# One K tile with rows of 64 KB in a decode kernel: fewer, larger loads, and the buffers that wait for them

## Chip, cores and metric

The kernel runs on one core of one Trainium2 chip, alone on that chip. The metric is the device time of one execution in microseconds.

## The reference, cut to what matters

```python
# x: [2, 1, 512]; k_cache, v_cache: [2, 32, 8192, 128] bf16, 134 MB each; wq [512, 4096], wo [4096, 512]
q = (layernorm(x) @ wq) per head
p = softmax(q . k * 128**-0.5)          # one query row per batch and head, 8192 keys
h = x + (p @ v) @ wo
out = h + relu_gated_ffn(layernorm(h))  # W_gate, W_up [512, 1376], W_down [1376, 512]
```

Almost all bytes are the two caches. Each is read once, with one multiply-add per element and query.

Of the kernel before, what the change touches and what calls it, by code (L numbers as in the profile page):

```python
# [8 lines left out]
BF16 = mybir.dt.bfloat16  # L9
# [30 lines left out]
def bass_sequential_preLN__gqa_block_cached__glu_gated_reglu__decode_kernel(  # L40
# [16 lines left out]
    DC = D // 128  # L57
# [22 lines left out]
    with ExitStack() as es:  # L80
# [15 lines left out]
        v_sem = [S(f"v{i}") for i in range(2)]  # L96
# [9 lines left out]
        K = [sb(f"K{i}", [128, SLOT], BF16) for i in range(2)]  # L106
# [14 lines left out]
        onesn = sb("onesn", [128, 128], BF16)  # L121
        scr = prod[:].rearrange("p j d -> p (j d)")
# [46 lines left out]
        def k_rows(p):  # L169
            hq, b = divmod(p // 2, B)  # L170
            return A_k_cache[b, A * hq:A * hq + A].rearrange(
                "h (p k j) d -> k (h p) (j d)", p=128 // A, k=2)[p % 2]

        def v_rows(o):
            hq, b = divmod(o, B)
            return A_v_cache[b, A * hq:A * hq + A].rearrange("h (p j) d -> (h p) (j d)", p=128 // A)

        def tile(x, p):
            return x[:].rearrange("p (k j d) -> p k j d", j=J, d=Dh)[:, p % 2 if x is V else 0]

        if True:

            def program():

                def load_k(p):
                    nc.sync.dma_start(K[p % 2][:], k_rows(p)).then_inc(k_sem[p % 2], 16)

                def load_v(o, k0, k1, sem):
                    nc.sync.dma_start(V[:, k0 * Dh:k1 * Dh], v_rows(o)[:, k0 * Dh:k1 * Dh]).then_inc(sem, 16)
# [5 lines left out]
                load_k(0)  # L195
                load_k(1)
# [104 lines left out]
                for r in range(2):  # L301
# [16 lines left out]
                load_v(0, 0, 2 * J, v_sem[0])  # L318
                nc.sync.dma_start(
                    X[:], A_wo[0:128 * DR].rearrange("(p r) n -> p (r n)", r=DR)).then_inc(sem_wo, 16)  # L320
# [41 lines left out]
                nc.tensor.sem_inc(v_sem[1], 16 * (NI - 1))  # L362
# [12 lines left out]
                body = Tokens(pe.count)  # L375

                def k_part(T, p, ev, k_wait):
                    k_t = tile(K[p % 2], p)
# [3 lines left out]
                    def score(g):  # L382
                        wait(a2p, ev[g])
                        kv_ = kT[g % 2][:].rearrange("p (k n r) -> p k r n", n=128, r=2)
                        for k in range(GT // 2):
                            jj = g * GT + 2 * k
                            for r in range(2):
# [3 lines left out]
                                if loop and g == NG - 2 and k == r == 0:  # L391
                                    T.mark(("kf", p), i)
# [23 lines left out]
                def pv(T, p, parts, between=None):  # L416
# [18 lines left out]
                    T.mark(("pv", p), i)  # L435
# [24 lines left out]
                with nc.Fori(0, NI, engines=OrderedEngineSet([nc.tensor.engine])):  # L460
                    k_part(body, 0, (1, 2, 3, 4), ((k2p, 1),))
                    collect(body, 6)
                    k_part(body, 1, (8, 9, 10, 11), ((k2p, 2),))
                    pv(body, 0, ((JC, J, ((v_sem[0], 16),)), (0, JC, ())))
                    pv(body, 1, ((JC, J, ((v_sem[1], 16), (a2p, 12))), (0, JC, ((a2p, EV),))))
# [4 lines left out]
                    for sem in v_sem:  # L470
                        nc.tensor.sem_inc(sem, -16)
                    nc.tensor.sem_inc(k2p, -2)
# [4 lines left out]
                tail = Tokens(0)  # L477
# [12 lines left out]
                pv(tail, P0, ((JC, J, ((v_sem[0], 16),)), (0, JC, ((a2p, 13),))))  # L490
# [64 lines left out]
                def q_copy(o):  # L555
                    if o == 0:
                        pool.wait(t_q2, t_q_b)
                    else:
                        pool.wait(tokp("fp", 2 * o - 2), (d2s, 2 * o))
                    nc.gpsimd.tensor_copy(out=q_c[:], in_=q_all[:, o]).then_inc(g2d, 1)  # L560

                def k_mult(p):
                    return nc.vector.tensor_tensor(  # L563
                        out=prod[:, 0:JC, :], in0=tile(K[p % 2], p)[:, 0:JC, :],
                        in1=q_c[:, Q2:QW].unsqueeze(1).broadcast_to([128, JC, Dh]), op=ALU.mult)

                def k_adds(p, run, last):
                    w = Dh
                    while w > 8:
# [3 lines left out]
                            out=prod[:, 0:JC, 0:w], in0=prod[:, 0:JC, 0:w], in1=prod[:, 0:JC, w:2 * w], op=ALU.add))  # L573
                    last()

                def k_reduce(p):
                    return nc.vector.tensor_reduce(  # L577
                        out=scores[p % PG][:, 0:JC], in_=prod[:, 0:JC, 0:8], axis=AX.X, op=ALU.add)
# [17 lines left out]
                with nc.Fori(0, NI, engines=OrderedEngineSet([nc.vector.engine])):  # L596
# [9 lines left out]

                    for q in range(PG):
                        if q == 0:
                            nc.vector.wait_ge(g2d, 1)
# [266 lines left out]
```

## The kernel before, the parts that the change touches

Work goes in 16 items. An item is one batch and four heads: 8 MB of K and 8 MB of V. The 128 partitions hold 256 positions each. K comes as two halves of 128 positions in two tiles, V as one tile of rows of 64 KB.

```python
K = [sb(f"K{i}", [128, SLOT], BF16) for i in range(2)]   # 32 KB a partition each
V = sb("V", [128, 2 * SLOT], BF16)                       # 64 KB a partition
X = sb("X", [128, DR * D], BF16)                         # wo, 28 KB a partition, loaded second after V(0)
prod = sb("prod", [128, JC, Dh], BF16)                   # 24 KB, VectorE's product
```

Of each half, VectorE makes the scores of positions 0 to 95 (product with q, four halving adds, a reduce). TensorE makes those of the other 32 (transposes, copies by ScalarE, matmuls). VectorE's loop body goes half by half:

```python
for q in range(PG):                       # the two halves
    if q == 0: nc.vector.wait_ge(g2d, 1)
    nc.vector.wait_ge(k_sem[q], 16)
    nc.vector.sem_inc(k2p, 1)             # lets TensorE start on this half
    run_d(k_mult(q))
    last_d(); nc.vector.sem_inc(d2s, 1)   # VectorE no longer needs this half of K
    k_adds(q, run_d, last_d)
    if q == 0:
        nc.vector.wait_ge(p2d, 1); normalize(Ob, run_d, last_d); run_d(o_scale(O_cur[:])); ...
    run_d(k_reduce(q))
    last_d(); nc.vector.sem_inc(d2a, 1)   # ScalarE may take the exps
```

SyncE issues each half of K as soon as VectorE and TensorE are through with the half that it replaces, and V when the last matmul on the old V is through:

```python
if p + 2 < NP:                             # p counts halves
    sp.wait((d2s, p + 1), tokp("kf", p))
    load_k(p + 2)
if p % 2 == 1 and p < P0 - 3:
    sp.wait(tokp("pv", p))
    load_v(p // 2 + 1, 0, 2 * J, v_sem[0])
# ... the last two items come in pieces (cut)
```

The softmax here doesn't subtract the row's maximum and nothing guards it: scores larger than these inputs give would overflow.

## Time and profile before

| What | Before |
|---|---|
| time, median of the first 3 runs | 658.9 us (658.81 to 659.58) |
| one period of the loop (an item) | 38.78 us in every one of 13 periods, to 0.01 |
| bytes of a period, and rate | 16.78 MB, 432.6 GB/s |
| VectorE busy in a period | 28.8 us |

Ways to read it: the row of DMA tenths tells how full the 16 DMA engines are. A transfer in the chain of waits is drawn from its issue to its landing, so most of a long one is time spent behind other transfers. In this text the "lead" of a load is the time from its issue to the landing of the load queued before it. The lines themselves are in the prediction.

### The profile page before, as it was taken

How to read it: one execution, taken by the hardware profiler on the slowest of the kernel's cores; microseconds unless marked ns; L12 is line 12 of the kernel's file. 1: busy time of each engine (PE TensorE's matmuls, PEld its weight loads, DVE VectorE, ACT ScalarE, POOL GpSimd, SP SyncE). 2: the span in 40 equal slices, each digit the busy share in tenths (PEclk: the TensorE clock that was granted, in tenths of full speed). 3: DMA queues.
4: the chain of work that ended last, by engine and by line, in shares of the span. 5: the costliest groups of instructions: out<-in, count | busy, mean ns of one | idle time of the engine just before them, and what ended most of it. 6: DMA issues, size and time to landing. Idle time of an engine off the chain costs nothing.

```text
span 657.5 us, 7820 instructions
## 1 busy us (share of the span) xinstructions
PE 306.7 (47%) x3096; PEld 202.9 (31%) x3097; DVE 469.1 (71%) x275; ACT 274.0 (42%) x687; POOL 25.5 (4%) x96
## 2 busy tenths in 40 slices
PE   2644345444354445436444443644445354445466
PEld 0331232323233232323314232331323233133234
DVE  1594594958949496794949769494985949589881
ACT  1642343433454254344424534442454435335271
POOL 4000000000000000000000000000000000002000
PEclk9856557655575755557565575756557575556676
DMA  9999999999999999999999999999999999999997
GB/s 383 422 437 430 437 439 419 470 391 447 425 462 433 403 447 415 470 397 439 445 419 458 403 447 417 443 441 423 443 419 462 405 437 447 417 429 433 429 421 310
DMA packets 8629, 281.17 MB, mean 428 GB/s; under 512 B 966, under 2 KB 1068, under 8 KB 1580
## 3 DMA queue, kind: packets, MB, share of 16 engines
q1 hardware_dynamic: 8612, 281.06, 99.3%
q8 instruction: 5, 0.08, 0.1%
q14 instruction: 4, 0.03, 0.0%
q10 hardware_dynamic: 8, 0.00, 0.0%
HBM read 281.05 MB, written 0.00 MB: 427 GB/s over the span
## 4 chain that ended last, share of the span: by engine, by line
DMA 80%; DVE 15%; PE 3%; issue 1%; ACT 0%; DVEq 0%; SPq 0%
DMA K<-in_A_k_cache_dram 69%; DVE prod L563 15%; DMA V<-in_A_v_cache_dram 5%; DMA K<-in_B_W_gate_dram 4%; DMA V<-in_A_wq_dram 2%; PE T L345 1%; PE O L428 1%; PE O L272 1%; ACT kT L589 0%; PE O L775 0%; PE O L827 0%; PE O L330 0%; PE Ob L440 0%; PE T L405 0%; DVE prod L281 0%
## 5 line engine op out<-in xcount | busy, mean ns | idle before, releaser
L563 DVE TENSOR_TENSOR prod<-K,q_c 128x12288 bf16<-128x12288 bf16 x32 | 209.9, 6558 | 146.7 <-DMA K<-in_A_k_cache_dram 136.0
L572 DVE TENSOR_TENSOR prod<-prod 128x6144 bf16<-128x6144 bf16 (+3 forms) x128 | 212.2, 1658 | 7.8
L405 PE MATMUL T<-ident_f,K 128*128 128x128 f32 x512 | 123.3, 403 | 134.6 <-DVEq L611 134.6
L589 ACT ACTIVATE kT<-T 128x1024 bf16<-128x1024 bf16 x128 | 127.1, 1022 | 122.7 <-PE T L405 118.7
L428 PE MATMUL O<-V,e 128*16 128x512 bf16 x1024 | 91.4, 533 | 111.8 <-DMA V<-in_A_v_cache_dram 111.8
L517 ACT ACTIVATE e<-scores 32x96 bf16<-32x96 f32 x128 | 53.9, 421 | 196.5 <-DVEq L625 193.3
L405 PEld LDWEIGHTS T<-ident_f,K 128*128 128x128 f32 x512 | 88.6, 206 | 137.6 <-DVEq L611 137.5
L428 PEld LDWEIGHTS O<-V,e 128*16 128x16 bf16 x1024 | 30.5, 117 | 165.3 <-DMA V<-in_A_v_cache_dram 113.3
L388 PE MATMUL S<-q_c,kT 128*128 128x8 bf16 x1024 | 48.6, 171 | 44.8 <-ACT kT L589 44.6
L388 PEld LDWEIGHTS S<-q_c,kT 128*128 128x128 bf16 x1024 | 41.9, 107 | 73.1 <-ACT kT L589 71.3
L440 PE MATMUL Ob<-sel,os_sb 128*128 128x4 f32 x136 | 30.2, 345 | 38.4 <-ACT os_sb L592 38.4
L440 PEld LDWEIGHTS Ob<-sel,os_sb 128*128 128x128 f32 x136 | 28.7, 312 | 40.3 <-ACT os_sb L592 40.2
L517 ACT ACTIVATE e<-S 32x32 bf16<-32x32 f32 x128 | 29.8, 233 | 16.1 <-PE S L388 15.0
L577 DVE TENSOR_REDUCE scores<-prod 128x96 f32<-128x768 bf16 x32 | 30.5, 953 | 2.8
L517 ACT ACTIVATION_READ_ACCUMULATOR e<-scores 32x1 f32 x128 | 30.0, 235 | 0.0
L517 ACT ACTIVATION_READ_ACCUMULATOR e<-S 32x1 f32 x128 | 25.6, 200 | 1.5
L589 ACT ACT_TABLE_LOAD x15 | 19.2, 1283 | 0.3
L560 POOL COPY q_c<-q_all 128x144 bf16<-128x144 bf16 x16 | 7.5, 472 | 243.5 <-PE O L428 231.3
L592 ACT ACTIVATE os_sb<-O 128x512 f32<-128x512 f32 x17 | 10.1, 597 | 15.3 <-PE O L428 14.9
L544 POOL MEMSET O_l<- 128x32 bf16 x13 | 1.7, 130 | 299.8 <-DVEq L622 299.8
L281 DVE CAST prod<-O 128x512 bf16<-128x512 f32 x1 | 0.7, 692 | 11.0 <-PE O L272 11.0
L272 PE MATMUL O<-V,xlT 128*2 128x512 bf16 x32 | 3.4, 600 | 7.7 <-DMA V<-in_A_wq_dram 7.7
(103 smaller groups left out, 94.2 us busy)
## 6 DMA issues: line engine op xcount, KB each, us to landing
K<-in_A_k_cache_dram SPq DMA_DIRECT2D x32, 4096.0 KB, 29.2
V<-in_A_v_cache_dram SPq DMA_DIRECT2D x3, 4096.0 KB, 31.7
V<-in_A_wq_dram SPq DMA_DIRECT2D x1, 4096.0 KB, 12.3
X<-in_A_wo_dram SPq DMA_DIRECT2D x1, 3584.0 KB, 46.2
V<-in_A_v_cache_dram SPq DMA_DIRECT2D x1, 3072.0 KB, 23.1
K<-in_B_W_up_dram SPq DMA_DIRECT2D x1, 1376.0 KB, 23.6
K<-in_B_W_gate_dram SPq DMA_DIRECT2D x1, 1376.0 KB, 26.6
V<-in_A_v_cache_dram SPq DMA_DIRECT2D x1, 1024.0 KB, 25.2
```

Source lines behind the costliest of these rows:

```text
L272: mm = nc.tensor.matmul(Op[i][32 * t:32 * t + B, :], lhsT=lT[:, c * B:(c + 1) * B], rhs=wq[:, c, n:n + 512], start=(c == 0), stop=(c == DC ...
L388: i = nc.tensor.matmul(Sp[p % 2][:, A * jj:A * jj + 2 * A], lhsT=kv_[:, k, r, :], rhs=q_c[:, 2 * A * r:2 * A * r + 2 * A], start=(r == 0), ...
L405: i = nc.tensor.transpose(Tp[g % 2][:, k * 128:(k + 1) * 128], k_t[:, j:j + 2, :].rearrange("p j d -> p (j d)").bitcast(F32), ident_f[:])
L428: i = nc.tensor.matmul(Op[0][c:c + 16, :], lhsT=e_t[q][:, j // VJ, :], rhs=v_t[:, j:j + VJ, :].rearrange("p j d -> p (j d)"), start=(q == ...
L440: i = nc.tensor.matmul(Ob[:, 0:A], lhsT=os_sb[:, jj * Dh:(jj + 1) * Dh], rhs=sel[:, A * jj:A * jj + A], start=(jj == 0), stop=(jj == VJ - 1))
L517: i = nc.scalar.activation(out=e_t[q][h, j0 // VJ:j1 // VJ, :].rearrange("p g (j a) -> p g j a", a=A)[:, :, :, a], in_=src(h, a), func=ACT ...
L560: nc.gpsimd.tensor_copy(out=q_c[:], in_=q_all[:, o]).then_inc(g2d, 1)
L563: return nc.vector.tensor_tensor(out=prod[:, 0:JC, :], in0=tile(K[p % 2], p)[:, 0:JC, :], in1=q_c[:, Q2:QW].unsqueeze(1).broadcast_to([128 ...
L572: run(nc.vector.tensor_tensor(out=prod[:, 0:JC, 0:w], in0=prod[:, 0:JC, 0:w], in1=prod[:, 0:JC, w:2 * w], op=ALU.add))
L577: return nc.vector.tensor_reduce(out=scores[p % PG][:, 0:JC], in_=prod[:, 0:JC, 0:8], axis=AX.X, op=ALU.add)
L589: to_pe(nc.scalar.activation(out=kT[gg % 2][:], in_=Tp[gg % 2][:].bitcast(BF16), func=ACT.Copy))
L592: to_pe(nc.scalar.activation(out=os_sb[:], in_=Op[0][:], func=ACT.Copy))
```

## The change

The intent: K loads like V, 8 MB in one go with rows of 64 KB, which halves its packets. For this the whole K tile must come free at once. So VectorE makes both halves' products first. The second product needs a place, which is the tile of wo, and wo therefore loads near the end. ScalarE takes the exps of VectorE's scores of both halves last, so that TensorE's second half isn't held up behind them.

```diff
-        K = [sb(f"K{i}", [128, SLOT], BF16) for i in range(2)]
+        K = sb("K", [128, 2 * SLOT], BF16)
+        prods = [X[:, 0:JC * Dh].rearrange("p (j d) -> p j d", d=Dh), prod]
...
-                    for q in range(PG):
-                        if q == 0:
-                            nc.vector.wait_ge(g2d, 1)
-                        nc.vector.wait_ge(k_sem[q], 16)
-                        nc.vector.sem_inc(k2p, 1)
-                        ... (mult, adds, normalise if q == 0, reduce)
+                    nc.vector.wait_ge(g2d, 1)
+                    nc.vector.wait_ge(k_sem[0], 16)
+                    nc.vector.sem_inc(k2p, 1)
                     for q in range(PG):
+                        run_d(k_mult(q, prods[q]))
+                    last_d()
+                    nc.vector.sem_inc(d2s, 1)
+                    nc.vector.wait_ge(p2d, 1)
+                    normalize(Ob, run_d, last_d)
+                    ...
+                    for q in range(PG):
+                        k_adds(prods[q], run_d, last_d)
+                        run_d(k_reduce(q, prods[q]))
...
                         exp_pe(q)
                         if q == 0:
                             sums()
+                    for q in range(PG):
                         nc.scalar.wait_ge(d2a, q + 1)
                         exp_dve(q)
...
-                    if p + 2 < NP:
-                        sp.wait((d2s, p + 1), tokp("kf", p))
-                        load_k(p + 2)
+                    if p % 2 == 1 and p < P1:
+                        o = p // 2 + 1
+                        sp.wait((d2s, 2 * o - 1), tokp("kf", p))
+                        if o < NI:
+                            load(K, A_k_cache, o, k_sem[0])
+                            sp.wait(tokp("pv", p))
+                            load(V, A_v_cache, o, v_sem)
+                        else:   # last item: K half, wo into X, K half, V in pieces
+                            ...
```

More of the change, by code (lines that the diff above doesn't have):

```diff
@@ L95, in bass_sequential_preLN__gqa_block_cached__glu_gated_reglu__decode_kernel @@
         k_sem = [S(f"k{i}") for i in range(2)]
-        v_sem = [S(f"v{i}") for i in range(2)]
+        v_sem = S("v")
         a2p, k2p, l2p = S("a2p"), S("k2p"), S("l2p")
@@ L167, in bass_sequential_preLN__gqa_block_cached__glu_gated_reglu__decode_kernel, with kv_rows, load @@
         ZC = 64
-        def k_rows(p):
-            hq, b = divmod(p // 2, B)
-            return A_k_cache[b, A * hq:A * hq + A].rearrange(
-                "h (p k j) d -> k (h p) (j d)", p=128 // A, k=2)[p % 2]
-        def v_rows(o):
+        def kv_rows(cache, o):
             hq, b = divmod(o, B)
-            return A_v_cache[b, A * hq:A * hq + A].rearrange("h (p j) d -> (h p) (j d)", p=128 // A)
+            return cache[b, A * hq:A * hq + A].rearrange("h (p j) d -> (h p) (j d)", p=128 // A)
         def tile(x, p):
-            return x[:].rearrange("p (k j d) -> p k j d", j=J, d=Dh)[:, p % 2 if x is V else 0]
+            return x[:].rearrange("p (k j d) -> p k j d", j=J, d=Dh)[:, p % 2]
         if True:
             def program():
-                def load_k(p):
-                    nc.sync.dma_start(K[p % 2][:], k_rows(p)).then_inc(k_sem[p % 2], 16)
-                def load_v(o, k0, k1, sem):
-                    nc.sync.dma_start(V[:, k0 * Dh:k1 * Dh], v_rows(o)[:, k0 * Dh:k1 * Dh]).then_inc(sem, 16)
+                def load(x, cache, o, sem, k0=0, k1=2 * J):
+                    nc.sync.dma_start(
+                        x[:, k0 * Dh:k1 * Dh], kv_rows(cache, o)[:, k0 * Dh:k1 * Dh]).then_inc(sem, 16)
                 nc.scalar.dma_start(x_row, A_x[:, 0]).then_inc(sem_x, 16)
@@ L194, in program @@
                     wo_rows, A_wo[128 * DR:].rearrange("(p r) n -> p (r n)", r=4)).then_inc(sem_wl, 16)
-                load_k(0)
-                load_k(1)
+                load(K, A_k_cache, 0, k_sem[0])
                 pool.run(nc.gpsimd.memset(ident_f[:], 0.0))
@@ L317, in program @@
                 sp.wait(t_q)
-                load_v(0, 0, 2 * J, v_sem[0])
-                nc.sync.dma_start(
-                    X[:], A_wo[0:128 * DR].rearrange("(p r) n -> p (r n)", r=DR)).then_inc(sem_wo, 16)
+                load(V, A_v_cache, 0, v_sem)
                 t_mm, t_cp = {}, {}
@@ L361, in program @@
                                  start=True, stop=True)
-                nc.tensor.sem_inc(v_sem[1], 16 * (NI - 1))
                 EV = 13
@@ L373, in mark @@
                         self.at[key] = pe.run(inst)[1] - self.base
-                body = Tokens(pe.count)
+                body, tail = Tokens(pe.count), Tokens(0)
                 def k_part(T, p, ev, k_wait):
-                    k_t = tile(K[p % 2], p)
+                    k_t = tile(K, p)
                     wait = nc.tensor.wait_ge
@@ L390, in score @@
                                     rhs=q_c[:, 2 * A * r:2 * A * r + 2 * A], start=(r == 0), stop=(r == 1))
-                                if loop and g == NG - 2 and k == r == 0:
+                                if loop and p % 2 and g == NG - 2 and k == r == 0:
                                     T.mark(("kf", p), i)
@@ L434, in pv @@
                             n += 1
-                    T.mark(("pv", p), i)
+                    if T is tail or q:
+                        T.mark(("pv", p), i)
                 def collect(T, a):
@@ L462, in program @@
                     collect(body, 6)
-                    k_part(body, 1, (8, 9, 10, 11), ((k2p, 2),))
-                    pv(body, 0, ((JC, J, ((v_sem[0], 16),)), (0, JC, ())))
-                    pv(body, 1, ((JC, J, ((v_sem[1], 16), (a2p, 12))), (0, JC, ((a2p, EV),))))
+                    k_part(body, 1, (7, 8, 9, 10), ())
+                    pv(body, 0, ((JC, J, ((v_sem, 16),)), (0, JC, ((a2p, 12),))))
+                    pv(body, 1, ((JC, J, ()), (0, JC, ((a2p, EV),))))
                     z_sum(Ob)
@@ L469, in program @@
                     nc.tensor.sem_inc(l2p, -1)
-                    for sem in v_sem:
-                        nc.tensor.sem_inc(sem, -16)
-                    nc.tensor.sem_inc(k2p, -2)
+                    nc.tensor.sem_inc(v_sem, -16)
+                    nc.tensor.sem_inc(k2p, -1)
                     nc.tensor.sem_inc(a2p, -EV)
@@ L475, in program @@
                 pe.count = body.base + NI * n_body
-                tail = Tokens(0)
                 P0, P1 = NP - 2, NP - 1
@@ L489, in program @@
                 tail.mark("op", i)
-                pv(tail, P0, ((JC, J, ((v_sem[0], 16),)), (0, JC, ((a2p, 13),))))
+                pv(tail, P0, ((JC, J, ((v_sem, 16),)), (0, JC, ((a2p, 13),))))
                 nc.tensor.wait_ge(a2p, 14)
@@ L558, in q_copy, with k_mult, k_adds @@
                     else:
-                        pool.wait(tokp("fp", 2 * o - 2), (d2s, 2 * o))
+                        pool.wait(tokp("fp", 2 * o - 2), (d2s, 2 * o - 1))
                     nc.gpsimd.tensor_copy(out=q_c[:], in_=q_all[:, o]).then_inc(g2d, 1)
-                def k_mult(p):
+                def k_mult(p, pr):
                     return nc.vector.tensor_tensor(
-                        out=prod[:, 0:JC, :], in0=tile(K[p % 2], p)[:, 0:JC, :],
+                        out=pr[:, 0:JC, :], in0=tile(K, p)[:, 0:JC, :],
                         in1=q_c[:, Q2:QW].unsqueeze(1).broadcast_to([128, JC, Dh]), op=ALU.mult)
-                def k_adds(p, run, last):
+                def k_adds(pr, run, last):
                     w = Dh
@@ L572, in k_adds, with k_reduce @@
                         run(nc.vector.tensor_tensor(
-                            out=prod[:, 0:JC, 0:w], in0=prod[:, 0:JC, 0:w], in1=prod[:, 0:JC, w:2 * w], op=ALU.add))
+                            out=pr[:, 0:JC, 0:w], in0=pr[:, 0:JC, 0:w], in1=pr[:, 0:JC, w:2 * w], op=ALU.add))
                     last()
-                def k_reduce(p):
+                def k_reduce(p, pr):
                     return nc.vector.tensor_reduce(
-                        out=scores[p % PG][:, 0:JC], in_=prod[:, 0:JC, 0:8], axis=AX.X, op=ALU.add)
+                        out=scores[p % PG][:, 0:JC], in_=pr[:, 0:JC, 0:8], axis=AX.X, op=ALU.add)
                 def exp_pe(p):
@@ L605, in last_d @@
                             nc.vector.wait_ge(d2d, n_d[0])
+                    nc.vector.wait_ge(g2d, 1)
+                    nc.vector.wait_ge(k_sem[0], 16)
+                    nc.vector.sem_inc(k2p, 1)
                     for q in range(PG):
-                        if q == 0:
-                            nc.vector.wait_ge(g2d, 1)
-                        nc.vector.wait_ge(k_sem[q], 16)
-                        nc.vector.sem_inc(k2p, 1)
-                        last_d()
-                        run_d(k_mult(q))
-                        last_d()
-                        nc.vector.sem_inc(d2s, 1)
-                        k_adds(q, run_d, last_d)
-                        if q == 0:
-                            nc.vector.wait_ge(p2d, 1)
-                            normalize(Ob, run_d, last_d)
-                            run_d(o_scale(O_cur[:]))
-                            last_d()
-                            nc.vector.sem_inc(d2g, 1)
-                        run_d(k_reduce(q))
+                        run_d(k_mult(q, prods[q]))
[3 more added lines that the diff above has]
+                    normalize(Ob, run_d, last_d)
+                    run_d(o_scale(O_cur[:]))
+                    last_d()
+                    nc.vector.sem_inc(d2g, 1)
+                    for q in range(PG):
+                        k_adds(prods[q], run_d, last_d)
+                        run_d(k_reduce(q, prods[q]))
                         last_d()
                         nc.vector.sem_inc(d2a, 1)
-                    for sem, n in ((d2d, n_d[0]), (g2d, 1), (p2d, 1), (k_sem[0], 16), (k_sem[1], 16)):
+                        if q == 0:
+                            nc.vector.sem_inc(d2s, 1)
+                    for sem, n in ((d2d, n_d[0]), (g2d, 1), (p2d, 1), (k_sem[0], 16)):
                         nc.vector.sem_inc(sem, -n)
@@ L660, in program @@
                         dve.last()
-                        t_dm[p] = dve.run(k_mult(p))
-                        k_adds(p, dve.run, dve.last)
+                        t_dm[p] = dve.run(k_mult(p, prod))
+                        k_adds(prod, dve.run, dve.last)
                         if p == P0:
-                            dve.wait(tokp("pv", p - 2))
-                        t_s[p] = dve.run(k_reduce(p))
+                            dve.wait(tokp("pv", p - 1))
+                        t_s[p] = dve.run(k_reduce(p, prod))
                         if p == P0:
@@ L697, in program @@
                         exp_dve(p)
-                    if p + 2 < NP:
-                        sp.wait((d2s, p + 1), tokp("kf", p))
-                        load_k(p + 2)
-                    if p % 2 == 1 and p < P0 - 3:
-                        sp.wait(tokp("pv", p))
-                        load_v(p // 2 + 1, 0, 2 * J, v_sem[0])
-                    elif p == P0 - 3:
-                        sp.wait(tokp("pv", p))
-                        load_v(NI - 1, 0, J, v_sem[0])
-                    elif p == P0 - 2:
-                        load_v(NI - 1, J, 2 * J, v_sem[1])
-                    elif p == P0 - 1:
-                        sp.wait(tokp("pv", p - 1))
-                        load_v(NI, 0, J, v_sem[0])
-                        sp.wait(tokp("pv", p))
-                        for k, (j0, j1) in enumerate(((V_LAST, J), (0, V_LAST))):
-                            load_v(NI, J + j0, J + j1, sem_vl[k])
+                    if p % 2 == 1 and p < P1:
[6 more added lines that the diff above has]
+                        else:
+                            load(K, A_k_cache, o, k_sem[0], 0, J)
+                            sp.wait((d2s, 2 * o))
+                            nc.sync.dma_start(
+                                X[:], A_wo[0:128 * DR].rearrange("(p r) n -> p (r n)", r=DR)).then_inc(sem_wo, 16)
+                            load(K, A_k_cache, o, k_sem[1], J, 2 * J)
+                            sp.wait(tokp("pv", p))
+                            load(V, A_v_cache, o, v_sem, 0, J)
+                            for k, (j0, j1) in enumerate(((V_LAST, J), (0, V_LAST))):
+                                load(V, A_v_cache, o, sem_vl[k], J + j0, J + j1)
                     if p == NP - 2:
@@ L719, in program @@
                             nc.sync.dma_start(
-                                K[0][:, k * DC * F:(k + 1) * DC * F],
+                                K[:, k * DC * F:(k + 1) * DC * F],
                                 w.rearrange("(p c) n -> p (c n)", c=DC)).then_inc(sem_w[k], 16)
@@ L723, in program @@
                             nc.sync.dma_start(
-                                K[0][:, 2 * DC * F + r0 * D:2 * DC * F + (r0 + n) * D],
+                                K[:, 2 * DC * F + r0 * D:2 * DC * F + (r0 + n) * D],
                                 B_W_down[r0 * 128:(r0 + n) * 128].rearrange("(p r) n -> p (r n)", r=n)).then_inc(sem_wd[k], 16)
@@ L758, in program @@
                     in1=Sp[0][:, 0:B].unsqueeze(1).broadcast_to([128, DC, B]), op=ALU.subtract))
-                wup, wgt = (K[0][:, k * DC * F:(k + 1) * DC * F].rearrange("p (c f) -> p c f", c=DC)
+                wup, wgt = (K[:, k * DC * F:(k + 1) * DC * F].rearrange("p (c f) -> p c f", c=DC)
                             for k in range(2))
-                wdn = K[0][:, 2 * DC * F:2 * DC * F + 10 * D].rearrange("p (r n) -> p r n", n=D)
+                wdn = K[:, 2 * DC * F:2 * DC * F + 10 * D].rearrange("p (r n) -> p r n", n=D)
                 pe.wait(t_d)
```

## The prediction

> **What bounds the kernel now.** I read the page's slices first, then the chain of waits, then one steady period of the loop in windows and in the timeline, and last the two ends of the span. The slices say what is full:
>
> ```profile
> DVE  1594594958949496794949769494985949589881
> DMA  9999999999999999999999999999999999999997
> GB/s 383 422 437 430 437 439 419 470 391 447 425 462 433 403 447 415 470 397 439 445 419 458 403 447 417 443 441 423 443 419 462 405 437 447 417 429 433 429 421 310
> DMA packets 8629, 281.17 MB, mean 428 GB/s; under 512 B 966, under 2 KB 1068, under 8 KB 1580
> ```
>
> The reader is to see that the DMA row is 9 in every slice but the last, while VectorE, the busiest engine, is between. The chain of waits, in order of time, repeats one piece from 72.9 us to 577.0 us, here for two rounds and for its end:
>
> ```profile
> 189.36 6.57 DVE prod L563
> ...
> 196.00 32.02 DMA K<-in_A_k_cache_dram
> ...
> 228.14 6.57 DVE prod L563
> ...
> 577.17 6.57 DVE prod L563
> ...
> 583.81 0.33 SPq L186
> 584.14 0.06 issue
> 584.20 31.70 DMA V<-in_A_v_cache_dram
> 615.90 0.04 issue
> ```
>
> It looks as if VectorE's product (6.57 us) sat in a loop with the K load. It does not: those 32.02 us for 4 MB are mostly queueing behind what was issued earlier. One item (K as two 4 MB halves, V as 8 MB) takes 38.78 us, and the windows of one period, and of the one where V too came as two halves, show the DMA engines full throughout and VectorE at 28.8 of 38.78:
>
> ```profile
> 189.24:228.02 38.78, 16.70 (x174) 11.54 (x174) 28.79 (x15) 16.71 (x42) 1.02 (x5) 0.60 1.00 432
> 577.04:615.82 38.78, 15.73 (x136) 11.10 (x136) 36.66 (x17) 15.38 (x41) 3.73 (x5) 0.54 1.01 432
> ```
>
> (columns: stretch, its length, busy PE, PE load, DVE, ACT, POOL, granted clock, DMA share, GB/s). 16,777,216 bytes in 38.78 us are 432.6 GB/s. So bytes set the end, as long as the queue never runs dry. How deep it is shows in the timeline of the same period:
>
> ```profile
> 196.00 15.74 SPq L186 DMA_DIRECT2D K<-in_A_k_cache_dram  x2
> ...
> 218.36 4.91 PE L428 MATMUL O<-V,e 128*16 128x512 bf16 x64 [6.94 <-DMA V<-in_A_v_cache_dram]
> ...
> 223.31 0.33 SPq L189 DMA_DIRECT2D V<-in_A_v_cache_dram  x1
> ```
>
> K's first half is issued at 196.0 while V, landing at 218.3, is still in flight; V is issued at 223.3 with both halves of K still to come (the first lands at 228.0, the second 9.7 us later). There are always 10 to 22 us of work in the queue.
>
> **What the Trainium skill says.** (1) "DMA: Bandwidth & Descriptors", section "Where 436 GB/s comes from": 16 ports give 435.2 GB/s. The trace agrees: 432.6 is 99.4% of that, so better loads alone can win 0.6% at most. (2) Same page, "Why small descriptors are slow (HBM only)": a packet has a small fixed overhead that matters for descriptors of a few hundred bytes. At 32 and 64 KB the trace shows almost nothing of it (below). (3) "VectorE: DVE Perf Modes", section on the mode that packs two bf16 into one read: two results a cycle at 0.96 GHz. The product of 12,288 elements would then take 6.40 us; the trace has 6.558. Changing the buffer that it writes should not change that. (4) "SBUF — State Buffer", "Who interferes with whom": a VectorE instruction with two SBUF inputs and a GpSimd one that reads SBUF exclude each other. The trace of before cannot confirm it, as GpSimd's few instructions (0.13 to 0.30 us each) lie beside the reduce, which has one input.
>
> **The change part by part.**
>
> *Rows of 64 KB for K.* A period has per DMA engine 16 packets for K (8 per half) and 8 for V. Against the ceiling of 435.2 (38.55 us) the period loses 0.23 us, 0.23/24 = 9.6 ns a packet. A second view: the period with V in halves ended at 615.90 instead of 577.04 + 38.78 = 615.82, so 0.08 us for 8 more packets an engine, 10 ns each. The change takes away 8 packets an engine for each of 15 items (the last keeps its halves), and 8 more where V was split in item 14: 16 x 0.08 = 1.3 us gained, an estimate.
>
> *wo moves from second in the queue to the end.* 3.67 MB take 8.5 us of the queue wherever they stand. Nothing starts on it before the tail. 0 us.
>
> *Order of VectorE.* Same instructions: two products, eight adds, two reduces, three small ones. 0 us of work, but their order now sets when buffers come free, and the queue is shallower, as the whole 8 MB of K are held until both halves are used. I lay one new period out from the moment K lands (0), with the durations of the old one.
> - K free for VectorE: start 0.12, two products of 6.56 back to back: 13.3.
> - K free for TensorE: first half's transposes and scores as now (0.09 to 6.2), exps to 8.2, copy of the sums to 8.8, collect to 10.7 (in the old period at 228.02 it ran 236.84 to 238.71), and the last transposes of the second half are through when its third score group starts, 4.67 after its own start (228.11 to 232.78): 15.4. Today the second half waits for VectorE; now it need not.
> - So K(next) is issued at about 15.45. V lands at 19.4 (8.39 MB at 432.6 GB/s). An issue must come ahead of the landing before it by start plus completion latency: the first load of the kernel took 12.32 us for 9.70 us of bytes, so 2.63. Deadline 16.75; slack 1.3 us.
> - V free: products to 13.3, normalise to 14.1, adds 6.8 and reduce 1.0 to 21.9, again to 29.8, exps of the second half 1.9 to 31.7 (old: 257.98 to 259.83), last 24 matmuls in four column groups, 6 x 0.43 = 2.6 at half clock, and V(next) is issued at 34.6 (33.3 at full clock). K lands at 38.75, deadline 36.1; slack 1.5 us.
>
> Both slacks are positive, so the queue still never runs dry: 0 us lost, and the period stays about 38.7.
>
> *The ends.* At the start K's first data is whole at 33.8 instead of 24.1, but VectorE had 9 us of idle per period and V is issued as before at 16.6. At the end the order is K first half, wo, K second half, V in pieces, weights; wo is issued 22 us after the landing of item 14's K, with 7 us of queue left, V's first part at 34.6 with 12 us left. The second half of K still lands 19.4 us before the last V piece (VectorE needs 6.6 + 6.7 + 1.0 and exps 1.9 = 16.2), and the feed-forward weights come last as now, landing at about 655. 0 us.
>
> Sum: 658.9 - 1.3 = 657.6; I keep back 0.2 for jitter in the thin slacks: 657.8 us.
>
> **The rivals.**
> 1. *The queue runs dry once a period*, at the issue of K or of V. For it: slacks of 1.3 and 1.5 us beside sums of 15 and 35 us, and a latency measured once, on an empty machine. GpSimd's reads (point 4 above) now lie beside adds with two SBUF inputs and could hold VectorE up by 0.5 to 0.8 us. Against it: the adds are not on the path to K's release, and V's slack takes 0.8. Each microsecond of deficit costs some 14 to 15 us: 1 us late makes 672.
> 2. *Larger rows are worth more*, near the ceiling: 15 x 0.23 = 3.5 us, so 655.4. Against it: K's 4 MB landed 9.7 us after V did, at the same rate as V's 64 KB rows.
> 3. *VectorE becomes the bound*, now that both products come ahead of everything. It has 28.8 of 38.78 us and starts with K's landing; its last reduce at 29.8 leaves 9 us. Against the clock it is safe: 0 us.
>
> **Range and chances.** Without a dry queue the time lies in 655.5 to 659.5, and the ceiling rules out a gain of 2% (646). A partial shortage of 0.2 to 0.3 us a period would give 661 to 662. For 2% slower (672) a deficit of 0.9 us in all periods is needed, that is an error of over 2 us in my layout: 8%. Range 656.0 to 662.0; faster 0.01, same 0.91, slower 0.08.
>
> **What would show it right or wrong.** Right: a period of 38.7 between K landings, DMA share 1.00 in each, SyncE issuing K about 15.5 and V 33 to 34.6 after a landing, products at 6.56. Wrong: periods above 38.8 with a DMA share below 1.00; then the lateness of the K issue (after 16.8) or of the V issue (after 36.1) says which slack was mis-sized, and if both issues are on time, the latency of 2.63 was. A period below 38.6 would speak for rival 2.

## The result, and the profile after

The changed kernel took 668.9 us (median of 6 runs, 664.8 to 670.9), against 658.9 (658.5 to 659.6, 6 runs). The ratio is 1.014, with a 95% interval of 1.011 to 1.017. Ratios here are the mean time of one kernel's fast runs over that of the other's in the same rounds, so they are not quite the ratio of the medians. The loss is under 2%, but beyond the noise and outside the predicted range. The runs also scatter over 6 us where those of before scatter over 1. The profiled execution took 666.1 us, among the faster ones.

The page hardly shows it: the DMA row is the same row of nines. The packets have fallen as intended, and the chain of waits has changed its make-up. First the page before, then the page after:

```profile
DMA 80%; DVE 15%; PE 3%; issue 1%; ACT 0%; DVEq 0%; SPq 0%
```

```profile
DMA packets 6324, 281.16 MB, mean 423 GB/s; under 512 B 710, under 2 KB 812, under 8 KB 1324
DMA 60%; PE 21%; ACT 12%; DVE 4%; issue 1%; SPq 0%; DVEq 0%; ACTq 0%
```

Before, DMA and VectorE's product alternated in the chain, and the DMA's part was queueing. Now the chain goes through TensorE and ScalarE, whose transposes, copies and exps set when K is issued. The time itself is seen in the windows of single periods of the changed kernel (from one landing of K to the next; columns as in the prediction):

```profile
35.06:75.46 40.40, 20.13 (x174) 12.51 (x174) 28.71 (x15) 16.48 (x42) 0.43 (x1) 0.50 1.01 427
75.46:114.17 38.71, 19.92 (x174) 12.53 (x174) 28.71 (x15) 16.64 (x42) 5.46 (x3) 0.54 0.99 422
114.17:153.50 39.33, 20.13 (x174) 12.49 (x174) 28.70 (x15) 16.64 (x42) 5.87 (x5) 0.50 1.00 427
153.50:193.87 40.37, 20.13 (x174) 12.50 (x174) 28.72 (x15) 16.64 (x42) 5.46 (x5) 0.54 1.01 425
...
428.53:467.27 38.74, 20.13 (x174) 12.50 (x174) 28.72 (x15) 16.64 (x42) 5.46 (x5) 0.50 1.00 433
```

The shortest period, 38.70 us, is what was predicted. But it is not every period: the 14 range up to 40.4, and their mean is 39.27. VectorE has the same 28.7 us in each. The DMA share says 1.00 even in a period of 40.4 us. That is the trap of this view: a packet that takes longer than it need counts as busy.

The timeline of the first of these periods (products of VectorE, issues of SyncE, the first matmul on V):

```profile
35.17 6.56 DVE L552 TENSOR_TENSOR X<-K,q_c 128x12288 bf16<-128x12288 bf16 x1 [14.54 <-DMA K<-in_A_k_cache_dram]
41.64 6.55 DVE L552 TENSOR_TENSOR prod<-K,q_c 128x12288 bf16<-128x12288 bf16 x1
...
50.37 0.33 SPq L182 DMA_DIRECT2D K<-in_A_k_cache_dram  x1
54.29 1.03 PE L418 MATMUL O<-V,e 128*16 128x512 bf16 x8 [2.69 <-DMA V<-in_A_v_cache_dram]
...
69.39 0.33 SPq L182 DMA_DIRECT2D V<-in_A_v_cache_dram  x1
75.58 6.56 DVE L552 TENSOR_TENSOR X<-K,q_c 128x12288 bf16<-128x12288 bf16 x1 [10.82 <-DMA K<-in_A_k_cache_dram]
```

K landed at 35.06, and the next K was issued 15.31 us later (15.47 in the following periods; predicted 15.45). V was issued 34.33 us after the landing (predicted 33.3 to 34.6). Both issues were on time by the prediction's layout. K's lead was 54.25 - 50.37 = 3.88 us, and in this period it was not enough: K landed 21.2 us after V, where 8 MB take 19.35. V's lead, in a period without loss, is 38.70 - 34.33 = 4.37 us.

The trace also holds the time at which each of the 16 DMA engines reports each transfer, and the start and duration of each packet. Summed over the 14 periods, K landed 7.0 us later than 19.35 after V, and V 1.1 us later than 19.35 after K. So 86% of the loss is at K. Landings of one transfer over its 16 engines, as offsets from the last in us (from the trace's records):

```
before, K half at 266.80   -2.06 -1.91 -1.90 -1.85 -1.84 -1.83 -1.81 -1.76 -1.73 -1.63 -1.60 -1.54 -1.48 -1.38 -0.38 0
before, K half at 305.57   -2.05 -1.91 -1.88 -1.85 -1.84 -1.82 -1.80 -1.75 -1.71 -1.63 -1.59 -1.51 -1.46 -1.37 -0.37 0
after,  V at 54.25         -1.79 -1.73 -1.65 -1.64 -1.63 -1.61 -1.40 -1.38 -1.37 -1.36 -1.35 -1.34 -1.32 -1.29 -1.26 0
after,  K at 75.46         -2.89 -2.73 -2.68 -2.65 -2.59 -2.46 -2.16 -2.10 -2.03 -1.72 -1.58 -1.55 -1.26 -0.97 -0.95 0
```

Before, the engines end up to 2 us apart, but the pattern repeats to some 0.03 us from period to period. There every load of the loop is issued 12.9 us or more ahead, so no engine waits. After, the pattern changes from one transfer to the next. The packet records around the issue at 50.37 show how. The engines finish V between 52.00 and 53.79, most of them before 52.5. The first packet of the new K starts at 52.16 (1.8 us after the issue). About half of the engines go on with K at once, and the others have to wait, the last of them until 53.57 (3.2 us after the issue). And of the 27 packets that start between 52.15 and 56.3, 20 take over 2.5 us, up to 3.69, instead of 2.42. Of the packets of 64 KB, 261 of 3,840 are long (over 2.5 us) in the changed kernel, 1 of 1,792 in the kernel before, and 25 of 3,840 in run e5 below, which has the same packets. The long packets hold most of the loss: what packets took beyond 2.42 us comes to 0.48 us per engine and period in the changed kernel and 0.07 in e5, while the periods differ by 0.57. That leaves some 0.15 us for waiting, an estimate.

One more thing moved that costs nothing. GpSimd's groups before and after:

```profile
L549 POOL COPY rsel<-rows 128x112 bf16<-128x112 bf16 x14 | 3.9, 276 | 32.4 <-DVEq L622 31.6
L551 POOL TENSOR_TENSOR O_l<-O_cur,mask 128x32 bf16<-128x32 bf16 x14 | 3.4, 241 | 0.0
```

```profile
L538 POOL COPY rsel<-rows 128x112 bf16<-128x112 bf16 x14 | 44.1, 3150 | 35.0 <-DVEq L607 34.1
L540 POOL TENSOR_TENSOR O_l<-O_cur,mask 128x32 bf16<-128x32 bf16 x14 | 25.0, 1785 | 0.0
```

The same instructions take 3.15 us instead of 0.28, since they now lie beside VectorE's adds, which have two inputs in SBUF. The Trainium skill's page "SBUF — State Buffer", section "Who interferes with whom", says that two such instructions contend. Here it is GpSimd that is held up, and not VectorE, whose 28.7 us a period are unchanged.

### The profile page after: what moved, and what is told of

Its sections match the earlier page's. It is cut to its first block, busy times and chain, and to the rows that moved or that the text cites. A ratio compares the mean times of both kernels' runs of the same rounds, so it can differ in the third digit from the quotient of the medians.

```text
span 664.9 us, 7713 instructions
## 1 busy us (share of the span) xinstructions
PE 339.6 (51%) x3096; PEld 210.9 (32%) x3097; DVE 467.9 (70%) x275; ACT 273.2 (41%) x687; POOL 85.6 (13%) x96
## 4 chain that ended last, share of the span: by engine, by line
DMA 60%; PE 21%; ACT 12%; DVE 4%; issue 1%; SPq 0%; DVEq 0%; ACTq 0%
DMA K<-in_A_k_cache_dram 55%; PE T L395 12%; ACT kT L578 7%; DMA K<-in_B_W_down_dram 5%; PE Ob L431 4%; ACT e L506 4%; PE S L378 4%; ACT os_sb L581 1%; DVE prod L561 1%; DVE X L561 1%; DVE X L552 1%; DVE prod L552 1%; PE O L418 0%; DVE scores L566 0%; SPq L713 0%
## 5 line engine op out<-in xcount | busy, mean ns | idle before, releaser
L552 DVE TENSOR_TENSOR X<-K,q_c 128x12288 bf16<-128x12288 bf16 x15 | 98.4, 6559 | 150.0 <-DMA K<-in_A_k_cache_dram 150.0
L418 PE MATMUL O<-V,e 128*16 128x512 bf16 x1024 | 114.3, 611 | 156.8 <-ACT e L506 112.6
L395 PE MATMUL T<-ident_f,K 128*128 128x128 f32 x512 | 131.3, 424 | 75.1 <-DVEq L598 69.9
L395 PEld LDWEIGHTS T<-ident_f,K 128*128 128x128 f32 x512 | 98.2, 224 | 77.2 <-DVEq L598 72.0
L561 DVE TENSOR_TENSOR prod<-prod 128x6144 bf16<-128x6144 bf16 (+1 forms) x68 | 112.7, 1658 | 5.5 <-DVE scores L566 3.7
L552 DVE TENSOR_TENSOR prod<-K,q_c 128x12288 bf16<-128x12288 bf16 x17 | 111.4, 6552 | 3.6 <-DMA K<-in_A_k_cache_dram 2.8
L561 DVE TENSOR_TENSOR X<-X 128x6144 bf16<-128x6144 bf16 (+3 forms) x60 | 99.5, 1659 | 3.8
L538 POOL COPY rsel<-rows 128x112 bf16<-128x112 bf16 x14 | 44.1, 3150 | 35.0 <-DVEq L607 34.1
L540 POOL TENSOR_TENSOR O_l<-O_cur,mask 128x32 bf16<-128x32 bf16 x14 | 25.0, 1785 | 0.0
L566 DVE TENSOR_REDUCE scores<-prod 128x96 f32<-128x768 bf16 x17 | 16.2, 953 | 0.6
```

Source lines behind the costliest of these rows:

```text
L395: i = nc.tensor.transpose(Tp[g % 2][:, k * 128:(k + 1) * 128], k_t[:, j:j + 2, :].rearrange("p j d -> p (j d)").bitcast(F32), ident_f[:])
L418: i = nc.tensor.matmul(Op[0][c:c + 16, :], lhsT=e_t[q][:, j // VJ, :], rhs=v_t[:, j:j + VJ, :].rearrange("p j d -> p (j d)"), start=(q == ...
L538: e.tensor_copy(out=rsel[:, :, o % B, :], in_=bass.AP(x.tensor, x.offset, [list(x.ap[0]), [DR - OS, A], [1, DR]]))
L540: e.tensor_tensor(out=w, in0=O_cur[:].unsqueeze(2).broadcast_to([128, A, NM]), in1=mask[:, off // 4:off // 4 + OS // 4 * (A - 1) + 1:OS // ...
L552: return nc.vector.tensor_tensor(out=pr[:, 0:JC, :], in0=tile(K, p)[:, 0:JC, :], in1=q_c[:, Q2:QW].unsqueeze(1).broadcast_to([128, JC, Dh] ...
L561: run(nc.vector.tensor_tensor(out=pr[:, 0:JC, 0:w], in0=pr[:, 0:JC, 0:w], in1=pr[:, 0:JC, w:2 * w], op=ALU.add))
```

## The experiments

Theory A: a load issued less than about 4.5 us ahead of the landing before it lets some DMA engines run dry. They restart late and with slow packets, and the lateness is no longer the same on each engine, so the slowest engine of one transfer is held up by another's delay in the next. Theory B: the transfers with rows of 64 KB are at fault by their size. Theory C: VectorE's new order or GpSimd's long instructions slow the transfers. Each experiment is the changed kernel with the edit shown. All gave correct results.

| Run | Time, median (range) in us | Ratio to before (95%) |
|---|---|---|
| changed kernel | 668.9 (664.8 to 670.9) | 1.014 (1.011 to 1.017) |
| e1 K as two transfers, same moment | 668.7 (665.7 to 675.1) | 1.018 (1.013 to 1.023) |
| e2 K's first half early | 661.2 (660.8 to 666.6) | 1.004 (1.002 to 1.006) |
| e3 K issued one score group later | 675.8 (673.6 to 679.3) | 1.025 (1.021 to 1.030) |
| e4 collect behind the second half | 660.9 (658.6 to 661.6) | 1.002 (1.000 to 1.004) |
| e5 e4, and normalise last | 657.9 (657.7 to 658.3) | 0.998 (0.997 to 1.000) |
| e6 e4, and V's first half early | 659.3 (658.9 to 660.5) | 1.001 (1.000 to 1.002) |
| e7 only V's first half early | 666.1 (663.8 to 670.2) | 1.011 (1.008 to 1.014) |
| e8 e6 with K as two transfers | 660.0 (659.8 to 660.3) | 1.002 (1.000 to 1.003) |

The kernel before ran beside them at 658.9 us. Runs e1 to e4 and e5 to e8 shared a chip each.

### e1: rows of 32 KB, issued at the same moment

```diff
-                            load(K, A_k_cache, o, k_sem[0])
+                            load(K, A_k_cache, o, k_sem[0], 0, J)
+                            load(K, A_k_cache, o, k_sem[0], J, 2 * J)
     (the same for item 0; VectorE waits for 32 instead of 16)
```

> Changed kernel, but K of an item comes as two transfers of 32 KB rows issued one right behind the other at the point where the one of 64 KB rows was issued. Theory A (the issue comes too late: 3.9 us ahead of the landing of V for the slowest DMA engine and about 2 us for the fast ones, so engines run dry and restart slowly): the issue time is the same, so still slow, 666 to 672 us, K periods 39.0 to 40.4. Theory B (the rows of 64 KB are the cause, by their size): back to 658 to 660 us, every period 38.78.

668.7 us: as slow as the changed kernel. (Its interval straddles 2%, so it is unclear whether it is slower by that much; slower than before it is.) One of its long periods:

```profile
113.30:153.17 39.87, 19.95 (x174) 12.54 (x174) 28.71 (x15) 16.65 (x42) 5.46 (x5) 0.54 1.00 422
```

K has the packets of the kernel before again, and the loss is still there. Theory B falls. The moment of issue and the new order of the engines (theory C) are left.

### e2: the first half of K issued early

```diff
                     for q in range(PG):
                         run_d(k_mult(q, prods[q]))
-                    last_d()
-                    nc.vector.sem_inc(d2s, 1)
+                        last_d()
+                        nc.vector.sem_inc(d2s, 1)
...
+                            sp.wait((d2s, 3 * o - 2), tokp("kf", p - 1))
+                            load(K, A_k_cache, o, k_sem[0], 0, J)
+                            sp.wait((d2s, 3 * o - 1), tokp("kf", p))
+                            load(K, A_k_cache, o, k_sem[0], J, 2 * J)
```

> As the run before, but the first half of K is issued as soon as its product and its transposes are done, about 6.8 us after K has landed, and the second half at 15.5 us as before. Theory A: the queue never has less than 12 us ahead of it when K's first half is issued, so no engine runs dry at K: 658.5 to 661 us, most periods 38.78. Theory B cannot tell it from the run before (both 32 KB rows, about 659). A third theory C, that the slow packets come of the new order of VectorE or of GpSimd's longer instructions, would leave it at 666 or more.

661.2 us, just over the expected 658.5 to 661; one of the five runs, the profiled one, took 666.6. VectorE's order and GpSimd's long instructions (87.6 us busy in this run, 85.6 in the changed kernel) are those of the changed kernel, so theory C does not explain most of the loss of the changed kernel. What was not expected is where the rest lies. The stretch from V to K, then the one from K to V, then a bad one from K to V:

```profile
54.45:73.86 19.41, 8.08 (x70) 2.46 (x70) 10.10 (x9) 4.60 (x17) 0.51 (x1) 0.50 1.02 435
73.86:93.65 19.79, 12.04 (x104) 10.04 (x104) 19.09 (x8) 12.05 (x25) 5.16 (x2) 0.50 0.98 422
229.83:250.85 21.02, 12.05 (x104) 10.05 (x104) 20.26 (x9) 12.04 (x25) 4.90 (x4) 0.50 0.96 407
```

K is nearly clean now; the late ones are the V loads, whose lead in this run was 4.2 us (issue at 69.67, K whole at 73.86). So V's lead is marginal as well.

### e3: K issued one score group later

```diff
-                                if loop and p % 2 and g == NG - 2 and k == r == 0:
+                                if loop and p % 2 and g == NG - 1 and k == r == 0:
                                     T.mark(("kf", p), i)
```

> Changed kernel with the K issue held back by one more score group, about 1.15 us (16.6 instead of 15.47 us after the landing of K). Theory A: the lead falls from 3.9 to about 2.7 us, and nearly all of the 1.15 us is lost in each of 14 to 15 periods: 678 to 688 us, K periods 39.8 to 40.8. Theories B and C, in which the lead plays no part: 666 to 671 us.

675.8 us, 6.9 more than the changed kernel; the mean period in the trace is 40.04 instead of 39.27. Two of them:

```profile
75.01:114.89 39.88, 18.96 (x174) 11.63 (x174) 28.72 (x15) 16.43 (x42) 5.47 (x3) 0.67 0.99 421
114.89:154.93 40.04, 20.14 (x174) 12.51 (x174) 28.70 (x15) 16.65 (x42) 5.62 (x5) 0.50 0.99 419
```

The sign is theory A's: K came about 1.0 us later (51.95 - 35.49 = 16.46 us after its landing), and no other theory knows of it. The size was overrated: 678 to 688 was expected, with nearly all of the delay lost in each period, and 0.5 to 0.8 us a period were. Why a part of the delay is not lost was not followed up. Not all of the loss is at K, either: the 14 V loads of the loop, with leads of 5.05 to 6.71 us, still landed up to 0.46 us late.

### e4: K free sooner, rows of 64 KB kept

```diff
                     k_part(body, 0, (1, 2, 3, 4), ((k2p, 1),))
-                    collect(body, 6)
                     k_part(body, 1, (7, 8, 9, 10), ())
+                    collect(body, 6)
     (VectorE: the p2d wait and the normalising go behind the first half's adds)
```

> Changed kernel with rows of 64 KB kept, but TensorE does the second half's transposes and scores ahead of the collect matmuls, and VectorE normalises after the first adds. K should be issued about 13.5 us after its landing (then VectorE's second product sets it), a lead of 5.9 instead of 3.9 us. Theory A: loss at K nearly gone, what is left is at V (lead 4.4 us, unchanged): 657.5 to 661 us, most periods 38.7. Theory B or C: 666 to 671 us.

660.9 us. K is issued 13.24 us after its landing, a lead of 6.1 us or more, and all K loads of the loop land 19.33 to 19.47 us after V. The loads of V, whose lead was left at 4.4 us, still slip in some periods:

```profile
54.49:73.84 19.35, 8.09 (x70) 2.46 (x70) 9.69 (x11) 4.60 (x17) 0.31 (x1) 0.59 1.03 431
73.84:93.67 19.83, 11.88 (x104) 9.97 (x104) 19.46 (x6) 11.94 (x25) 0.00 (x0) 0.50 0.98 423
93.67:113.02 19.35, 8.08 (x70) 2.44 (x70) 9.25 (x10) 4.60 (x17) 0.77 (x3) 0.50 1.00 434
```

First and third line: V to K. Second: K to V, 0.48 us late.

### e5: V issued sooner too

```diff
     (on top of e4)
                     for q in range(PG):
                         k_adds(prods[q], run_d, last_d)
                         if q == 0:
                             nc.vector.wait_ge(p2d, 1)
-                            normalize(Ob, run_d, last_d)
-                            run_d(o_scale(O_cur[:])) ...
                         run_d(k_reduce(q, prods[q]))
                         ...
+                    normalize(Ob, run_d, last_d)
+                    run_d(o_scale(O_cur[:])) ...
+                    nc.vector.sem_inc(n2p, 1)      # z_sum on TensorE waits for it: same PSUM bank
```

> Run e4 left its losses at the V loads alone (every K load landed 19.35 us after V, V loads 19.35 to 19.83 us after K); V was issued 34.3 us after K landed, 4.4 us ahead of the next landing. Here the normalising (0.75 us of VectorE) goes behind the last reduce, so V should be issued at 33.6 us, 5.1 us ahead, and rows stay 64 KB for K and V. Theory A: losses at V shrink to nearly none: 657.6 to 659.3 us, nearly all periods 38.70. Rival (what is left in e4 is a random loss of some transfers, whatever their lead): 660 to 661.5 us as e4.

657.9 us, the fastest of all and 0.16% under the kernel before (interval 0.9972 to 0.9997), with runs within 0.6 us of each other. It is also what the prediction gave for the change (657.8), now that both leads are longer. The issues and two periods:

```profile
48.47 0.33 SPq L182 DMA_DIRECT2D K<-in_A_k_cache_dram  x1
68.85 0.33 SPq L182 DMA_DIRECT2D V<-in_A_v_cache_dram  x1
```

```profile
35.24:73.94 38.70, 19.71 (x174) 12.21 (x174) 28.70 (x15) 16.40 (x42) 0.31 (x1) 0.59 1.00 434
...
538.41:577.11 38.70, 19.97 (x174) 12.42 (x174) 28.72 (x15) 16.55 (x42) 0.97 (x5) 0.50 1.00 434
```

V is issued 33.61 us after the landing of K instead of 34.34, a lead of 5.09 us, and the slips are gone: 14 periods of 38.69 to 38.73. So what was left in e4 was not random: 0.7 us of VectorE's work, moved from before the issue to after it, was the rest of the loss.

### e6: V's first half early instead

```diff
     (on top of e4)
+                            sp.wait(tokp("pv", p - 1))
+                            load(V, A_v_cache, o, v_sem, 0, J)
                             sp.wait(tokp("pv", p))
-                            load(V, A_v_cache, o, v_sem)
+                            load(V, A_v_cache, o, v_sem1, J, 2 * J)
```

> Run e4 with V as two transfers of 32 KB rows, the first issued as soon as the first half's matmuls are through (about 27 us after K's landing, a lead of over 11 us), the second at 34.3 us with the first still queued. K keeps its rows of 64 KB. Theory A: no engine runs dry any more: 658.2 to 659.3 us, all periods 38.78 with a spread under 0.1, like the kernel before. Rival of random losses: 660 or more.

659.3 us, at the upper end of the expected range; the trace is clean:

```profile
35.12:73.92 38.80, 19.90 (x174) 12.45 (x174) 28.70 (x15) 16.40 (x42) 0.98 (x1) 0.50 1.00 432
73.92:112.71 38.79, 19.75 (x174) 12.31 (x174) 28.70 (x15) 16.55 (x42) 0.77 (x3) 0.59 1.00 433
```

The mean of 14 periods is 38.78. Against e5's 38.70 this is V's 8 more packets an engine.

### e7: V's first half early, K as in the change

The edit of e6 on the changed kernel itself.

> Changed kernel with only V split and its first half issued early, K left at its lead of 3.9 us. In the trace of the changed kernel 86% of the lost time lay in the K loads. Theory A: most of the loss stays, 664 to 668 us, and all of it at the K landings. If instead V's lead was what made K late as well, it would fall to 659.

666.1 us, as expected: a deep lead for V alone leaves most of the loss. The stretches from V's landing to K's:

```profile
54.64:74.12 19.48, 6.87 (x62) 2.33 (x62) 9.98 (x8) 4.60 (x17) 0.00 (x0) 0.59 0.99 426
132.94:152.96 20.02, 7.06 (x62) 2.36 (x62) 9.60 (x8) 4.60 (x17) 0.67 (x1) 0.59 0.95 411
```

Not quite all of it is at K, as was expected: a few second halves of V came 0.2 to 0.4 us late too. They had been issued 14 us and more ahead of the landing before them, so no engine can have run dry there. Theory A does not explain these small losses. In e6 and e8, where V is issued as early and K is on time, there are none.

### e8: e6 with K in rows of 32 KB

> Run e6 with K too as two transfers of 32 KB rows, issued together at the same point. Nothing runs dry in either, so this against e6 is the worth of the rows of 64 KB for K: the prediction said 8 packets an engine less, 10 ns each, 0.08 us for each of 15 items, 1.2 us in all. Expected 1.0 to 1.5 us slower than e6, periods 38.86 instead of 38.78.

660.0 us, 0.7 more than e6 by the medians. By the traces, which scatter less, a period is 38.86 against 38.78:

```profile
35.24:74.11 38.87, 17.83 (x174) 10.64 (x174) 28.71 (x15) 16.27 (x42) 1.59 (x1) 0.68 1.00 432
74.11:112.97 38.86, 19.53 (x174) 12.45 (x174) 28.70 (x15) 16.53 (x42) 0.77 (x3) 0.54 1.00 433
```

This is the worth of K's larger rows by itself: 0.075 us a period, 1.1 us over 15.

## Why the prediction was right or wrong

- **The bound: right.** The kernel stays a stream of bytes; with long enough leads (e5, e6, e8) a period is 38.70 to 38.86 us whatever the order of the compute engines.
- **Rows of 64 KB: right.** 0.08 us a period was predicted; e6 against e8 gave 0.075 and e5 against e6 0.08. Rival 2 (3.5 us in all) falls.
- **Order of VectorE, wo at the end, GpSimd: right that they cost no time.** The layout of the period was met: K issued at 15.2 to 15.5 us (15.45 predicted), V at 34.3 (33.3 to 34.6). Wo took 8.5 to 8.8 us of the queue in its new place, 8.5 in its old one. Rival 1 feared that GpSimd could hold VectorE up, and the prediction held that the trace of before could not tell. That reading missed an instruction: one GpSimd copy of 16, at 599.81 us, lay beside VectorE's adds and took 3.00 us instead of 0.30, while the four adds took their usual 6.74.
- **The deadline: wrong, and this is the step that failed.** "An issue must come ahead of the landing before it by start plus completion latency: the first load of the kernel took 12.32 us for 9.70 us of bytes, so 2.63. Deadline 16.75; slack 1.3 us." The lead of 2.63 us was mis-sized. Runs with leads of 3.9 (changed kernel, at K) and 4.2 to 4.4 us (e2, e4, at V) lost time, though not at every load; with 5.1 (e5, at V) and 6.1 us (e4 and e5, at K) a load was late by 0.12 us at most. So the need lies between 4.4 and 5.1 us where the other loads are on time, and the slacks of 1.3 and 1.5 us were really shortages of up to 1.2 and 0.7. Once other loads have come late it is no sharp line: in the changed kernel the V load issued at 228.21, 5.06 us ahead, landed 0.87 us late.
- **What the term left out, in part argued.** The landing of a transfer is that of its slowest engine. The others finish up to 2 us sooner and have that much less lead: 3.88 - 1.8 = 2.1 us for the fastest in the first period shown, under 2.63 even by the prediction's own figure. Adding the spread of 2 us to 2.63 gives 4.6, an estimate inside the measured bracket. The packets add that a restart beside running traffic took up to 3.2 us from issue to first byte, against 1.8 at the very start (the first load, issued at 0.81, had its last engine going at 2.58). But the lead of the fastest engine does not tell which loads are hit: with 0.98 us (K issued at 90.93) nothing was lost, with 2.73 (K issued at 404.79) 0.51 us. Nor does waiting: at the V load of 228.21 no engine waited over 0.6 us, and yet 15 of its first 16 packets took over 2.5 us, up to 3.19.
- **Rival 1 came nearest,** in its weaker form: a partial shortage, 0.57 us a period in the trace (39.27 against 38.70), not in all periods alike. It came out as the prediction's last section had it: "if both issues are on time, the latency of 2.63 was" the mis-sized term. The sign named beside it, a DMA share below 1.00, was no help: the long periods show 0.98 to 1.01. That a queue that runs short costs mostly longer packets, and little idle time, is not in the prediction. At 14 periods the loss is 8.0 us; less the 1.1 gained, 6.9 of the 7.4 us between the two profiled spans. The median run is 10.0 us slower than before; such a one was not profiled.
- **What stays open.** Why packets are slow for one or two rounds after a late issue, also on engines that did not wait, and which periods are hit: in four of 14 nothing was lost at the same leads. The experiments show that the short lead is the cause, but not by which mechanism. The records do not say which engine a packet ran on.

## What to carry to other kernels

In a kernel bound by its loads, count for each load how long before the landing of the one ahead of it is issued, and keep that lead well above the start latency of an empty queue: 2.6 us by the first load was too little here, 5 us were enough only while every load was on time, and some 13 us left no loss in the kernel before. A longer lead is worth more than larger rows: merging two buffers into one saves a packet overhead of 0.2% and takes away the early release that kept the queue deep. If a lead is short, move work that does not release the buffer to after the issue (e4, e5) before splitting anything, and read landings, since the DMA's busy share stays at 1.00 while its packets grow longer.

## What the Trainium skill lacked or had wrong

- "DMA: Bandwidth & Descriptors", section "Anatomy of one DMA", gives a fixed cost of about 2.0 us per DMA (measured on the other issue path). It has no figure for the lead that a saturated queue needs: here over 4.4 and under 5.1 us while the other loads are on time. After running dry, an engine of the first long period started 1.8 to 3.2 us after the issue, with packets of up to 3.7 us instead of 2.42.
- No page gives the spread between the 16 engines of one transfer: 1.2 to 2.9 us in the loop of the changed kernel, and about 2.06 us with nearly the same pattern in every period of before, where no engine waits.
- "DMA: Bandwidth & Descriptors", section "Why small descriptors are slow (HBM only)", works out its overhead per packet for small descriptors only. From 32 to 64 KB the runs show 0.075 to 0.08 us for 8 packets an engine (and the one of 4 bytes that ends a transfer), about 10 ns a packet.
- "HBM Reference", section "Specifications", puts a core streaming alone at about 425 GB/s. In the loop the stream here ran at 432.6 (before) and 433.5 (e5: 16.78 MB in 38.70 us), near the 435.2 of the DMA page; over its whole span the kernel before read 427.
- "SBUF — State Buffer", "Who interferes with whom", was right that the two contend: GpSimd's copy went from 0.28 to 3.15 us beside VectorE's adds, which kept their times.
- No page gives the cost of an instruction fetch to the loads: a packet of 16 KB takes about 1.0 us of one DMA engine. In the kernel before one lies at 24.9 us, and the packet after it took 1.69 us instead of 1.22. K's landings over the engines are 0.57 us apart before it (24.11) and 2.09 after it (35.33).
